# Weights enter the conversion at 0.8 chunks a slot, in place of 0.4, while the first eight heads run alone

## The chip, the cores and the metric

The kernel runs on one core of a Trainium2 chip. The metric is the device time of one execution in microseconds (us); lower is better. Times are given as the median of several runs.

## What is computed

Causal attention with a gate of cumulative sums for 4 batches of 8 heads (576 positions, head dimension 64), then two dense two-layer blocks on the 2304 resulting tokens (512 to 2048 to 512 each). All matrices arrive as 64-bit or 32-bit floats, and the result is asked for in near-float32 accuracy.

```python
scores = scale * q @ k.T + minimum(-(cum[:, None] - cum[None, :]), 0)   # causal
x = softmax(scores) @ v                          # 4 x 8 heads -> 2304 x 512
h = x @ w1_in;  x = (h * clip(h + 3, 0, 6) / 6) @ w1_out
h = x @ w2_in;  y = (h * sigmoid(h)) @ w2_out
```

## The kernel before

**Heads.** Attention is cut into 64 parts, called heads here: the first 256 rows ("A") or the rest ("B") of one head of one batch. The first 22 are handled "whole" (L484, L503, L516, L546, L610, L617, L628): scores on PE (tiles ps0, ps1), mask and row minimum on DVE into pb0 and pb1 (L503), exponential on ACT (L516), transposes on PE (pt, L546), a copy on ACT (th), the product with the values on PE (po, L610), normalizing on DVE (L617), and for each pair of heads a transpose back (px, L628) and a copy to xA on DVE (L107). The inputs of the first 14 heads lie in SBUF places that weights take over later (`spare`).

**Steps.** The first dense block runs in steps. Step i (counted from 0) makes one 128-wide slice of h for 256 tokens in `first` (12 matmuls, L239 to L241, into ph, of which there is one buffer), gates it in `gate_high` and `gate_low` (ACT L251, DVE L252, a copy to gh at L107, DVE L259), and adds its share to the sums in `second` (12 matmuls, L278 to L280). The L252 of a step is called its gate here: it is the last reader of ph, so the next step's `first` can't begin before it. Gate 1 is that of step 0. The first 16 steps use heads 0 to 7.

**Weights.** Each weight matrix comes as 16 chunks of 512 KB (128 x 512 numbers of 64 bits), 32 for the first block, in the order i0, o0, i1, o1, and so on. A chunk passes the `Feed`: load by DMA (L132), two ACT instructions (`fields`, L144 and L145), three on DVE (`join`, L153, L157, L160), a rounding copy on ACT (`high`, L105) and a subtraction on DVE (`low`, L171). Step i needs i chunk number i in `first` and o chunk number i one step later in `second`. After the L171 of its chunk a weight is ready. One `tick` moves each chunk in the feed one stage further and loads one more.

**Order of the work.** The program is written as a plan of slots. Slots 0 to 8 hold heads only (eight heads, and a ninth slot that finishes them); from slot 9 on a slot holds a step, and nearly always a head. In each slot `rate` chunks enter the feed: `feed_at` gathers the fraction over the four places of a slot where `ticks` stands, and its whole part is ticked. Three ticks are made before slot 0. A scheduler then sets the order of each engine's instructions with its own idea of their costs, so the program's order only leads it: steps and heads of different slots are interleaved. Each engine runs its own instructions strictly in the order it was given.

```python
for i in range(4):
    feed_at += rate / 4
    tk[i] = int(feed_at)
    feed_at -= tk[i]
slot(cur, p1, p2, nx, loads, has_step, tk)
```

Of the kernel before, what the change touches and what calls it, by code (L numbers as in the profile page):

```python
# [27 lines left out]
def kernel(  # L28
# [17 lines left out]
    B, H, D, S = qT.shape  # L46
# [281 lines left out]
    def split_rows():  # L328

        def row(tag, name):  # L330
            return wpool.tile([BH, S], F32R, tag=tag, name=name)

        f = NF - 1
        hi, lo = row(f"i{f}", "cumh"), row(f"o{f}", "cuml")
        one, neg = row(f"i{NF // 2 - 2}", "one"), row(f"o{NF // 2 - 2}", "neg")
        nc.gpsimd.memset(f32(one), 1.0)
        nc.gpsimd.memset(f32(neg), -1.0)
        nc.scalar.copy(hi, crow)
        nc.vector.tensor_tensor(out=lo, in0=crow, in1=f32(hi), op=ALU.subtract)
        for r, t in enumerate((one, one, hi, lo, neg, neg)):  # L340
            nc.sync.dma_start(f32(rows_d[:, r, :]), f32(t))
# [294 lines left out]
    def split1(blk):  # L636

        n = sizes[blk][1]
        b, a, _ = blocks[blk][0]
        xhs, xls = [], []  # L640
        for c in range(NDC):
            xh = xpool.tile([P, n], F32R, tag=f"xh{c}", name=f"xh{blk}_{c}")
            xl = xpool.tile([P, n], F32R, tag=f"xl{c}", name=f"xl{blk}_{c}")
            srcs = [((xB if a else xA)[b, c], slice(0, T1))]
            if n > T1:
                srcs += [(xZ[c], slice(T1, n))]
            for src, o in srcs:
                nc.scalar.copy(xh[:, o], src)
                nc.vector.tensor_tensor(
                    out=xl[:, o], in0=src, in1=f32(xh[:, o]), op=ALU.subtract  # L650
                )
            xhs.append(xh)
            xls.append(xl)
        xsplit[blk] = [(xhs, xls)]
# [39 lines left out]
    def slot(cur, p1, p2, nx, loads, mm, tk=(0, 0, 0, 0)):  # L694

        nonlocal step
        ng = len(p1.groups) if p1 else 0
        npc = len(cur.pieces) if cur else 0

        def scores(i):  # L700
            if i < npc:
                cur.score(i)
                cur.soft(i)

        def exps(i):
            if i < npc:
                cur.expo(i)

        def transposed(i):
            if i < ng:  # L710
                p1.trans(i)
                p1.trans_low(i)

        scores(0)
        scores(1)
        exps(0)
        if p2:
            p2.av_sum()
        ticks(tk[0])
        if mm:  # L720
            first(step, 0)
        if p1:
            p1.v_high()
        exps(1)
        scores(2)
        if nx:
            nx.qk_high()
        transposed(0)
        if p1:
            p1.v_low()  # L730
        exps(2)
        if cur:
            cur.load_v()
        if nx and npc <= 3:
            nx.qk_low()
        ticks(tk[1])
        if mm:
            first(step, 1)
            gate_high(step)
        scores(3)  # L740
        if nx and npc > 3:
            nx.qk_low()
        exps(3)
        for hd in loads:
            hd.load()
        transposed(1)
        if cur:
            cur.norm()
        ticks(tk[2])
        if mm:  # L750
            second(step - 1, 0)
        transposed(2)
        if mm:
            gate_low(step)
        transposed(3)
        ticks(tk[3])
        if nx:
            nx.places()
        for hd in loads:
            hd.load_cum()  # L760
        if mm:
            second(step - 1, 1)
        if p1:
            p1.av()
        if mm:
            step += 1

    def at(i):
        return heads[i] if 0 <= i < len(heads) else None
# [13 lines left out]
    nslot = 0  # L783
    for has_head, has_step in plan:
        cur = at(k) if has_head else None
        nx = at(k + 1) if has_head else None
        loads = []
        while has_head and loaded < len(heads) and loaded <= k + (
            2
        ):  # L790
            loads.append(heads[loaded])
            loaded += 1
        k += has_head and cur is not None
        tk = [0, 0, 0, 0]
        if not feed.done():
            rate = ((0.4,)*9+(2,))[min(nslot, len(((0.4,)*9+(2,))) - 1)]
            for i in range(4):
                feed_at += rate / 4
                tk[i] = int(feed_at)
                feed_at -= tk[i]  # L800
        slot(cur, p1, p2, nx, loads, has_step, tk)
        if nslot == 2:
            split_rows()
        p1, p2 = cur, p1
        nslot += 1
        if nslot == H + 1:
            p2.av_sum()
            p2 = None
            split1(0)
            turns["s"] = turns["s"][:1]  # L810
        if has_step and step in first_step[1:NB1]:
            blk = first_step.index(step)
            assert k - (cur is not None) >= (blk + 1) * H
            if p2:
                p2.av_sum()
                p2 = None
            if blk == NB1 - 1:
                cx.close()
                xpool = c0.enter_context(
                    tc.tile_pool(name="xlast", bufs=1, side="right", reuse_waits="tile")  # L820
                )
            split1(blk)
            if blk == NB1 - 1:
                break
# [335 lines left out]
```

## Time and profile before

| | us |
|---|---|
| median of 3 runs (lowest, highest) | 1031.37 (1030.43, 1031.85) |
| profiled execution, its time | 1032.36 |
| profiled execution, its span (first to last instruction) | 1030.6 |
| PE busy in the span | 993.1 (96%) |
| weight loads of PE (PEld) | 921.9 (89%) |
| DVE busy | 720.5 (70%) |
| ACT busy | 523.4 (51%) |
| POOL busy | 204.8 (20%) |

The shares are means over stages that differ. In the first 150 us heads, weights and steps run side by side; after that PE has hardly a gap up to 600 us. All times in the trace count from the first instruction. A matmul's end is modelled, so the distance from one start to the next tells how fast PE really goes; on DVE, too, the next instruction often starts before the last one's end, and the distance of starts is the cost of one more instruction.

### The profile page before, as it was taken

How to read it: one execution, taken by the hardware profiler on the slowest of the kernel's cores; microseconds unless marked ns; L12 is line 12 of the kernel's file. 1: busy time of each engine (PE TensorE's matmuls, PEld its weight loads, DVE VectorE, ACT ScalarE, POOL GpSimd, SP SyncE). 2: the span in 40 equal slices, each digit the busy share in tenths (PEclk: the TensorE clock that was granted, in tenths of full speed). 3: DMA queues.
4: the chain of work that ended last, by engine and by line, in shares of the span. 5: the costliest groups of instructions: out<-in, count | busy, mean ns of one | idle time of the engine just before them, and what ended most of it. 6: DMA issues, size and time to landing. Idle time of an engine off the chain costs nothing.

```text
span 1030.6 us, 18218 instructions
## 1 busy us (share of the span) xinstructions
PE 993.1 (96%) x6322; PEld 921.9 (89%) x6322; DVE 720.5 (70%) x1794; ACT 523.4 (51%) x1138; POOL 204.8 (20%) x378
## 2 busy tenths in 40 slices
PE   4988999999999999999999999999999999999996
PEld 3878899999999999999998887789988899889895
DVE  6699986888788878888728896977574334743342
ACT  5697744555456666656516563755353223432232
POOL 5000033443245444444401231000000000000000
PEclk9999999999999999999999999999999999999999
DMA  4793131222222322321114956343354332442412
GB/s 151 210 339 122 48 93 43 57 75 59 87 61 63 88 68 62 88 73 56 52 41 143 375 218 225 121 174 132 126 188 165 127 143 81 175 154 81 143 72 61
DMA packets 51907, 124.78 MB, mean 121 GB/s; under 512 B 9972, under 2 KB 31464, under 8 KB 48488
## 3 DMA queue, kind: packets, MB, share of 16 engines
q1 hardware_dynamic: 51816, 123.63, 36.0%
q8 instruction: 50, 0.82, 0.3%
q14 instruction: 41, 0.34, 0.1%
HBM read 98.96 MB, written 24.63 MB: 120 GB/s over the span
## 4 chain that ended last, share of the span: by engine, by line
PE 85%; DVE 7%; DMA 3%; ACT 1%; POOL 1%; issue 1%; SPq 1%; DVEq 0%; POOLq 0%; ACTq 0%
PE ph L239 6%; PE ph L240 6%; PE a L981 6%; PE ph L241 6%; PE a L982 6%; PE a L983 6%; PE acc L279 6%; PE acc L280 6%; PE acc L278 6%; PE h L965 5%; PE h L967 5%; PE h L966 5%; PE poB L595 4%; PE pt0B L546 1%; DMA out_dram<-o 1%; PE pt1B L546 1%
## 5 line engine op out<-in xcount | busy, mean ns | idle before, releaser
L239 PE MATMUL ph<-xh,wi 128*128 128x256 f32 (+1 forms) x512 | 155.4, 304 | 6.0 <-DVE g L252 5.9
L279 PE MATMUL acc<-gl,wo 128*128 128x256 f32 (+1 forms) x512 | 153.5, 301 | 0.4 <-DVE gl L259 0.2
L240 PE MATMUL ph<-xl,wi 128*128 128x256 f32 (+1 forms) x512 | 153.1, 299 | 0.0
L241 PE MATMUL ph<-xh,wi 128*128 128x256 f32 (+1 forms) x512 | 152.9, 299 | 0.0
L280 PE MATMUL acc<-gh,wo 128*128 128x256 f32 (+1 forms) x512 | 151.2, 297 | 0.0
L278 PE MATMUL acc<-gh,wo 128*128 128x256 f32 (+1 forms) x512 | 146.0, 301 | 0.1
L1010 ACT ACTIVATE gh<-h 128x384 fp32r<-128x384 f32 x96 | 50.4, 525 | 177.7 <-DVE h L1018 177.5
L981 PE MATMUL a<-wo,gh 128*128 128x512 f32 x288 | 113.1, 393 | 2.4 <-ACT gh L1010 2.4
L982 PE MATMUL a<-wo,gh 128*128 128x512 f32 x288 | 113.1, 393 | 0.0
L239 PEld LDWEIGHTS ph<-xh,wi 128*128 128x128 f32 x512 | 98.3, 192 | 11.1 <-DVE g L252 6.6
L240 PEld LDWEIGHTS ph<-xl,wi 128*128 128x128 f32 x512 | 98.7, 193 | 2.9
L279 PEld LDWEIGHTS acc<-gl,wo 128*128 128x128 f32 x512 | 96.9, 189 | 4.8 <-DVE gl L259 1.4
L241 PEld LDWEIGHTS ph<-xh,wi 128*128 128x128 f32 x512 | 98.5, 192 | 2.8
L280 PEld LDWEIGHTS acc<-gh,wo 128*128 128x128 f32 x512 | 96.7, 189 | 3.7
L278 PEld LDWEIGHTS acc<-gh,wo 128*128 128x128 f32 x512 | 96.0, 189 | 4.3 <-DVE gh L107 0.4
L983 PE MATMUL a<-wo,gl 128*128 128x512 f32 x288 | 90.4, 395 | 0.0
L251 ACT ACTIVATE g<-ph,half 128x512 f32<-128x512 f32 (+1 forms) x80 | 51.3, 643 | 63.7 <-PE ph L241 63.1
L1012 DVE TENSOR_TENSOR gl<-h,gh 128x384 fp32r<-128x384 f32 x96 | 53.5, 557 | 40.7 <-ACT h L1011 38.7
L252 DVE SCALAR_TENSOR_TENSOR g<-g,ph 128x512 f32<-128x512 f32 (+1 forms) x80 | 50.5, 633 | 40.1 <-ACT g L251 39.9
L1018 DVE TENSOR_TENSOR h<-h,u 128x384 f32<-128x384 f32 x72 | 40.1, 557 | 53.1 <-PE h L967 52.7
L99 POOL TENSOR_SCALAR gh<-g 128x512 fp32r<-128x512 f32 x64 | 50.8, 794 | 126.0 <-DVE g L252 112.7
L965 PE MATMUL h<-x0t,w 128*128 128x384 f32 x192 | 65.6, 342 | 0.7 <-DVE u L1018 0.7
(224 smaller groups left out, 2563.3 us busy)
## 6 DMA issues: line engine op xcount, KB each, us to landing
w<-w_d SPq DMA_DIRECT2D x18, 1792.0 KB
w_d<-w SPq DMA_DIRECT2D x8, 1792.0 KB
k2B<-in_kT_dram SPq DMA_DIRECT2D x64, 144.0 KB
rawi<-in_w1i_dram SPq DMA_DIRECT2D x16, 512.0 KB
rawo<-in_w1o_dram SPq DMA_DIRECT2D x16, 512.0 KB
rawi<-in_w2i_dram SPq DMA_DIRECT2D x16, 512.0 KB
rawo<-in_w2o_dram SPq DMA_DIRECT2D x16, 512.0 KB
q2B<-in_qT_dram SPq DMA_DIRECT2D x64, 80.0 KB
```

Of the source, the lines that this page charges most:

```text
L239: nc.tensor.matmul(o, wih[:, cs], xh[c], start=c == 0, stop=False)
L240: nc.tensor.matmul(o, wih[:, cs], xl[c], start=False, stop=False)
L241: nc.tensor.matmul(o, wil[:, cs], xh[c], start=False, stop=c == NDC - 1)
L278: nc.tensor.matmul(a, woh[:, cs], gh[:, jj, :], start=b0, stop=False)
L279: nc.tensor.matmul(a, woh[:, cs], gl[:, jj, :], start=False, stop=False)
L280: nc.tensor.matmul(a, wol[:, cs], gh[:, jj, :], start=False, stop=b1)
L965: nc.tensor.matmul(ps, w[:, 0, cs], xh[:, c, :], start=c == 0, stop=False)
L966: nc.tensor.matmul(ps, w[:, 0, cs], xl[:, c, :], start=False, stop=False)
L981: nc.tensor.matmul(accs[t], gh[:, k, cs], woh, start=b0, stop=False)
L982: nc.tensor.matmul(accs[t], gh[:, k, cs], wol, start=False, stop=False)
L983: nc.tensor.matmul(accs[t], gl[:, k, cs], woh, start=False, stop=b1)
L1012: nc.vector.tensor_tensor(out=gl[:, i, o], in0=g, in1=f32(gh[:, i, o]), op=ALU.subtract)
```

## The change

```diff
         if not feed.done():
-            rate = ((0.4,)*9+(2,))[min(nslot, len(((0.4,)*9+(2,))) - 1)]
+            rate = 0.8 if nslot <= H else 2
             for i in range(4):
```

H is 8, so slots 0 to 8 are meant in both versions, and from slot 9 on the rate is 2 in both. In nine slots 0.4 gives 3.6, that is 3 ticks; 0.8 gives 7.2, that is 7. By slot 9 the feed has made 10 ticks in place of 6, and every chunk from the fourth on stands earlier in the program. No instruction is added or taken away; the scheduler's order changes on all engines up to about the 1500th of 6100 PE instructions and is the same behind that.

**DVE around gate 1.** Names carry the chunk or head before the tile's number. Before:

```order
L153 SCALAR_TENSOR_TENSOR rawi_5_688<-rawi_5_688 128x512
L171 TENSOR_TENSOR wi_4_811<-magi_4_726,wi_4_811 128x512
L157 TENSOR_SCALAR magi_5_813<-magi_5_813 128x512
L160 ISA mago_4_768<-rawo_4_640,mago_4_768 128x1024
L252 SCALAR_TENSOR_TENSOR g_542<-g_542,ph_522 128x256
L503 ISA pb0A_5_830,mxA_5_829<-ps0A_5_845,cmask 128x128
```

And with the change:

```order
L160 ISA mago_6_826<-rawo_6_693,mago_6_826 128x1024
L171 TENSOR_TENSOR wi_6_862<-magi_6_777,wi_6_862 128x512
L153 SCALAR_TENSOR_TENSOR rawo_7_784<-rawo_7_784 128x512
L503 ISA pb0A_5_874,mxA_5_873<-ps0A_5_889,cmask 128x128
L503 ISA mxA_5_873 128x1
L252 SCALAR_TENSOR_TENSOR g_586<-g_586,ph_555 128x256
```

The gate comes after the same 13 heads, but after the 13th L171 (i6) in place of the 9th (i4). Counted over all DVE instructions ahead of gate 1, the change has 5 more L153, 3 L157, 4 L160, 4 L171 and one 128-wide L503.

**DVE around gates 11 and 12, where the conversion ends.** Before, ahead of gate 12 (step 11):

```order
L160 ISA magi_14_1603<-rawi_14_1492,magi_14_1603 128x1024
L171 TENSOR_TENSOR wo_13_1632<-mago_13_1562,wo_13_1632 128x512
L617 TENSOR_TENSOR xtA_2_1481<-poA_3_1543,sums_96 128x2x64
L252 SCALAR_TENSOR_TENSOR g_1513<-g_1513,ph_1494 128x256
L430 TENSOR_TENSOR qsA_6_1718<-q2A_6_1593,qsA_6_1718 64x256
```

With the change, around gate 11 (step 10):

```order
L160 ISA mago_15_1612<-rawo_15_1508,mago_15_1612 128x1024
L523 TENSOR_SCALAR sums_92<-sums_92 128x2
L259 TENSOR_TENSOR gl_1298<-g_1296,gh_1297 128x256
L617 TENSOR_TENSOR xtA_2_1525<-poA_3_1583,sums_96 128x2x64
L252 SCALAR_TENSOR_TENSOR g_1385<-g_1385,ph_1352 128x256
L524 RECIPROCAL sums_92<-sums_92 128x2
L171 TENSOR_TENSOR wo_15_1678<-mago_15_1612,wo_15_1678 128x512
```

The same head work (xtA_2, from head 3 of the third batch) stands one gate earlier, and the last chunk, o15, is done right behind gate 11, where before only 25 of the 32 chunks are done by gate 11. Between gates 1 and 11 the change has on DVE 3 more 256-wide and 2 more 128-wide L503, 3 L523, 4 L524, 2 L617, 2 copies to xA, 2 casts to qs and 4 subtractions at L430 and L431, and of the conversion 5 fewer L153, and 1 L157, 1 L160 and 3 L171 more.

**SP, the loads of heads 3 and 4.** inA is the place of a head's inputs. Before:

```order
L399 DMA inA_2_157<-orow 1x16x16
L389 DMA inA_3_184<-in_qT_dram 64x256
...
L399 DMA inA_3_184<-orow 1x16x16
L389 DMA inA_4_217<-in_qT_dram 64x256
...
L132 DMA rawo_1_228<-in_w1o_dram 128x1024
L398 DMA inA_4_217<-cum_d 1x256
```

With the change (a line of dots stands for the head's other loads, here as above):

```order
L399 DMA inA_2_157<-orow 1x16x16
L132 DMA rawo_1_180<-in_w1o_dram 128x1024
L389 DMA inA_3_189<-in_qT_dram 64x256
...
L399 DMA inA_3_189<-orow 1x16x16
L132 DMA rawi_2_228<-in_w1i_dram 128x1024
L389 DMA inA_4_230<-in_qT_dram 64x256
...
L398 DMA inA_4_230<-cum_d 1x256
```

One chunk's load now stands ahead of head 3's loads, and two stand ahead of head 4's first.

## Rows read from the trace of the kernel before

**Rows 1.** Windows by stage: us of each engine busy (instructions), granted clock, DMA share, GB/s.

```profile
20.00:45.00 25.00, 23.95 (x96) 20.89 (x95) 15.18 (x62) 14.89 (x43) 0.00 (x0) 1.00 0.59 176
45.00:58.20 13.20, 12.34 (x48) 10.79 (x47) 13.04 (x41) 12.71 (x33) 0.00 (x0) 1.00 0.99 321
58.20:114.40 56.20, 50.01 (x349) 46.60 (x350) 56.20 (x162) 46.40 (x106) 4.35 (x14) 0.94 0.53 181
114.40:121.60 7.20, 6.30 (x55) 6.05 (x54) 7.18 (x26) 6.07 (x18) 0.87 (x1) 1.00 0.23 63
121.60:145.30 23.70, 22.23 (x183) 21.26 (x181) 21.95 (x71) 14.16 (x35) 4.94 (x8) 1.00 0.24 65
145.30:250.00 104.70, 104.70 (x870) 103.94 (x871) 80.83 (x236) 53.63 (x134) 45.03 (x79) 1.00 0.23 63
```

**Rows 2.** Timeline of PE: start, duration, instruction; neighbours at 60 and at 66 us.

```profile
60.12 0.41 PE L239 MATMUL ph<-xh,wi 128*128 128x256 f32 x1
60.34 0.41 PE L240 MATMUL ph<-xl,wi 128*128 128x256 f32 x1
...
66.04 0.28 PE L239 MATMUL ph<-xh,wi 128*128 128x256 f32 x1
66.16 0.28 PE L240 MATMUL ph<-xl,wi 128*128 128x256 f32 x1
```

**Rows 3.** Timeline of DVE around gate 1; the L252 is gate 1.

```profile
56.66 0.69 DVE L171 TENSOR_TENSOR wi<-magi,wi 128x512 fp32r<-128x512 f32 x1
57.27 0.43 DVE L157 TENSOR_SCALAR magi<-magi 128x512 int32<-128x512 int32 x1
57.60 0.69 DVE L160 CUSTOM_DVE_ANT_0 mago<-rawo,mago 128x1024 uint16<-128x1024 uint16 x1
58.20 0.42 DVE L252 SCALAR_TENSOR_TENSOR g<-g,ph 128x256 f32<-128x256 f32 x1
58.53 0.29 DVE L503 CUSTOM_DVE_ANT_0 pb0A<-ps0A,cmask 128x128 f32<-128x128 f32 x1
...
58.74 0.70 DVE L153 SCALAR_TENSOR_TENSOR rawo<-rawo 128x512 int32<-128x512 int32 x1
59.34 0.17 DVE L523 TENSOR_SCALAR sums<-sums 128x2 f32<-128x2 f32 x1
59.41 0.43 DVE L503 CUSTOM_DVE_ANT_0 pb1A<-ps1A,cmask 128x256 f32<-128x256 f32 x1
59.76 0.09 DVE L503 DVE_READ_ACCUMULATOR2_ANT mxA<- 128x1 f32 x1
```

**Rows 4.** Timeline of DVE: gate 11.

```profile
114.41 0.45 DVE L252 SCALAR_TENSOR_TENSOR g<-g,ph 128x256 f32<-128x256 f32 x1
```

**Rows 5.** Groups of ACT, 20 to 58.2 us: count, busy us, mean ns, idle before.

```profile
L144 ACT ACTIVATE rawo<-rawo 128x512 int32<-128x512 uint32 x5 | 3.4, 677 | 1.1 <-DMA rawo<-in_w1o_dram 1.1
```

**Rows 6.** Timeline of SP: the load of a weight chunk.

```profile
17.96 0.43 SPq L132 DMA_DIRECT2D rawo<-in_w1o_dram  x1
```

**Rows 7.** Waits of PE, whole span, for a gate: total us, times, longest.

```profile
PE ph L239 <- DVE g L252: 5.9, 7, 1.8
```

**Rows 8.** Timeline of PE: first matmuls of steps 11 and 17.

```profile
115.83 0.37 PE L239 MATMUL ph<-xh,wi 128*128 128x256 f32 x1
...
145.30 0.36 PE L239 MATMUL ph<-xh,wi 128*128 128x256 f32 x1 [0.27 <-DVE g L252]
```

**Rows 9.** Waits of PE, 114 to 150 us, columns as in rows 7.

```profile
PE pxA L628 <- DVE xtA L617: 0.9, 1, 0.9
PE ph L239 <- DVE g L252: 0.8, 2, 0.5
PE ps0A L492 <- DVE qsA L430: 0.4, 1, 0.4
PE acc L279 <- DVE gl L259: 0.2, 1, 0.2
```

**Rows 10.** Windows of 2 us, columns as in rows 1.

```profile
72.00:74.00 2.00, 2.00 (x12) 2.00 (x10) 2.00 (x6) 1.29 (x3) 0.00 (x0) 0.50 0.90 323
90.00:92.00 2.00, 2.00 (x12) 1.97 (x11) 2.00 (x8) 0.90 (x3) 0.00 (x0) 0.61 0.41 166
```

## The prediction, made before the changed kernel ran

> **What bounds the kernel now.** I read the windows by stage first [rows 1]. The reader is to see three regimes. From 20 to 45 us PE is busy 23.95 of 25.00 us and DVE only 15.18: the heads run alone and PE sets the pace. From 45 to 114 us DVE is full (13.04 of 13.20, then 56.20 of 56.20): the conversion of the weights, the heads and the steps meet there. From 145 us PE has no gap in 104.70 us. So whatever this change gives or takes must show before 145 us, and from there PE carries it to the end unchanged.
>
> PE's own pace in the first regime has to be read from the distance of starts [rows 2]. The column of the granted clock says 1.00 there, but at 60 us two 128x256 matmuls start 0.22 us apart, and at 66 us 0.12 us. The heads thus run at the lower of the two clock levels, 1.2 GHz, which is why a stage with so little in it fills PE.
>
> Then come the steps' gates. Gate 1 stands at 58.20 [rows 3], gate 11 at 114.41 [rows 4]. Ten gates take 56.2 us on a DVE without a gap.
>
> **What the change moves.** It does what it says: 13 chunks are converted ahead of gate 1 in the new order, 9 in the old. The cost of each instruction on DVE is the distance to the next start [rows 3]: L171 0.61, L157 0.33, L160 0.60, L153 0.60, the L503 of 128 columns 0.21 and of 256 columns 0.35, L523 0.07, L252 0.33.
>
> *Ahead of gate 1.* 5 x 0.60 + 3 x 0.33 + 4 x 0.60 + 4 x 0.61 + 0.21 = 9.0 us more on DVE. Between 20 and 58.2 us DVE was busy 15.18 + 13.04 = 28.22 of 38.20 us [rows 1], so 9.98 us lie idle, and with the change 37.2 of 38.2 are taken. ACT was busy 14.89 + 12.71 = 27.60; it gets about 12 more instructions of the conversion (three stages of four chunks), at most 0.68 each [rows 5], so at most 35.8. PE was busy 36.29. The idle time of DVE is therefore the cover for the moved work, and it just suffices, with three engines at 94 to 97%.
>
> Let d be the delay of gate 1. At the least DVE is the bound with no gap at all, and gate 1 comes 1.0 us earlier (d = -1.0). At the most nothing is hidden and d = 9.0. My value is near the low end, for the nearest row to a stage with full DVE is 45 to 58.2 us, and there PE still was busy 12.34 of 13.20, so it lost 6.5% against 4.2% between 20 and 45. That much over 25 us is 0.6 us. To this come two loads of weights that now stand ahead of the loads of heads 3 and 4 on SP, 0.43 us each [rows 6], 0.9 us, hidden only if those loads landed early; and 0.5 us, half of what DVE has left, for ACT's fuller queue. Sum: d = 2.0.
>
> *From gate 1 to gate 11.* DVE is full in both versions. By the counts of the two orders the change has there 3 x 0.35 + 2 x 0.21 + 3 x 0.07 + 4 x 0.07 + 2 x 0.21 for heads (L617 priced like the narrow L503) and 8 x 0.33 for copies, casts and subtractions (priced like L252), together 5.0, and for the conversion -5 x 0.60 + 0.33 + 0.60 + 3 x 0.61 = -0.2. So 4.8 us more: three more heads are fitted in, and the conversion stays as dense as it was, only further ahead. Gate 11 falls at 58.2 + d + 56.2 + 4.8 = 119.2 + d. **The steps come later in the middle, not earlier**: where `first` waited before, it was for the gate on DVE, 7 times [rows 7], and for no weight.
>
> *From gate 11 on* the conversion is over, where before seven more chunks were still to finish (4 L157, 5 L160, 7 L171, 8.6 us). Here DVE's cover is gone and PE sets the pace alone. Before, step 11 began at 115.83 and step 17 at 145.30 [rows 8], 29.5 us for 207 matmuls of the PE order, of which 2.3 us were waits, all for DVE [rows 9]. Without those it is 27.2 us, 0.131 a matmul. The change has 211 matmuls between the same two places: 27.6 us, from 119.6 + d (0.4 for the gate itself) to 147.2 + d. But at its step 17 it has done 28 matmuls more, those of one B head, 3.7 us at that pace, so it compares with 149.0 before. The balance is 1.8 us gained, less d.
>
> *After that* the order evens out and PE is full in both; I count nothing. The sum with d = 2.0: +0.2 us on the profiled execution's own 1032.36 (its span 1030.6 and 1.8 around it). The median of the runs lies 1.0 lower, at 1031.37, and gives 1031.6.
>
> One rule speaks against the change. What the rows show: after PE had stood waiting for gates, the granted clock fell to 0.50 and 0.61 in two places [rows 10], down to the 1.2 GHz level; there the 12 matmuls of a `first` cost 12 x (0.22 - 0.12) = 1.2 us more [rows 2], hidden so far because DVE was the bound. The Trainium skill, "TensorE: Matmul & The Clock Gate", section "What's actually happening", says that the throttled state is the default and that activity releases it. By that rule a PE that waits 4.8 us longer for its gates would fall back once more, and if that lasted past gate 11 the sum would be 1032.8 in place of 1031.6. The trace agrees that the clock falls after waits, but both its places lie well before gate 11, so my sum leaves it out.
>
> **The rivals.**
> 1. *The early heads jam* (slower). DVE, ACT and PE at 94 to 97% each, in fixed orders that the scheduler made with other costs, wait for each other: a chunk's L153 that stands ahead of a head's L503 holds up the head, and PE with it. Price: d itself, all of which stays, less 1.8. It decides from d = 3.9 (2.1 us slower, 0.2%); d = 5 gives 1034.6, d = 7 1036.6, d = 9 1038.6. For it: PE is cold and has no spare in 20 to 58 us. Against it: DVE's work is spread in pieces of 0.6 us, and scores run two heads ahead of the transposes.
> 2. *The cover holds fully* (faster). d = -1.0, a DVE without a gap from 20 us on: 1.8 + 1.0 = 2.8 us gained, 1028.6. For it: 45 to 58.2 us shows DVE at 99%. Against it: there PE had a lead, and it must feed DVE every head.
> 3. *The DVE time is worth its full price* (much faster). 8.6 us of conversion leave the stretch in which DVE is full, and the end moves by as much: 1022.8. Against it: PE has only 2.3 us of waits after gate 11 to give up [rows 9], and the order spends the room between the gates on heads.
>
> **How the numbers follow.** A measurement of this kernel tells about 0.2%, 2.1 us, from no change. My forecast, no change that can be measured, holds for d from -0.3 to 3.9: 0.46. Rival 1 beyond 3.9: 0.36, of which 0.04 for d somewhat below 3.9 with a fallen clock past gate 11. Rival 2: 0.15; rival 3: 0.03. The range runs from rival 2's 1028.6 to d = 7, 1036.6; outside are rival 3 and the last part of rival 1.
>
> **What would show it.** Gate 1 at about 60.2 us (58.2 and 62.1 bound the forecast); DVE busy over 90% between 20 and 58 us; gate 11 near 121 us, later than before; the last L171 near 122 us; no wait of PE for DVE between gate 11 and step 17, and step 17 near 149 us. I am wrong if gate 1 stands beyond 63 us, if PE waits after gate 11 for something that DVE had hidden (a load of a B head, POOL), or if gate 11 comes before 114 us.

## The result and the profile after

The change makes the kernel slower: 1036.36 us, median of eight runs (1035.71 to 1042.82), against 1031.26 us for the kernel before (eight runs, 1029.88 to 1032.59). The ratio is 1.0058, with a 95% interval of 1.0048 to 1.0068. The forecast was 1031.6 us; the measured time lies at the upper end of the range.

The profile that came with this result is of the slowest of the eight executions (1042.82 us). The rows below therefore come from a second profile of the same kernel, of an execution of 1036.94 us; its runs are the experiment e_again.

| us | before | after |
|---|---|---|
| profiled execution | 1032.36 | 1036.94 |
| its span | 1030.6 | 1035.2 |
| PE busy | 993.1 | 993.3 |
| DVE busy | 720.5 | 720.8 |
| ACT busy | 523.4 | 522.5 |

All engines do the same work in 4.6 us more. The windows by stage show where; each stage is cut at the places that were used before, gate 1 at 61.1, gate 11 at 125.2, the start of step 17 at 155.2 (columns as in rows 1).

```profile
20.00:45.00 25.00, 22.48 (x90) 19.80 (x88) 20.52 (x74) 18.72 (x54) 0.00 (x0) 1.00 0.69 202
45.00:61.10 16.10, 14.60 (x57) 12.69 (x57) 15.56 (x47) 15.77 (x38) 0.00 (x0) 1.00 0.99 315
61.10:125.20 64.10, 55.75 (x375) 52.20 (x376) 61.93 (x190) 49.22 (x118) 5.45 (x17) 0.89 0.42 140
125.20:155.20 30.00, 28.27 (x235) 27.61 (x234) 25.24 (x79) 15.68 (x42) 9.37 (x17) 1.00 0.23 65
155.20:250.00 94.80, 94.80 (x793) 94.17 (x792) 65.85 (x191) 44.96 (x110) 35.34 (x63) 1.00 0.19 55
```

Against [rows 1] the stretch from gate 1 to gate 11 has grown from 56.2 to 64.1 us. VectorE, full before (56.20 of 56.20, 162 instructions), now makes 190 instructions there in 61.93 us, and stands idle for 2.2. The granted clock of the stretch is 0.89 in place of 0.94. From 155 us on PE is full, as before.

The waits of PE in that stretch have changed their kind. This is the view of waits from 61.1 to 125.2 us:

```profile
PE acc L279 <- DVE gl L259: 2.8, 4, 1.5
PE acc L278 <- DVE gh L107: 2.2, 2, 2.0
PE poA L610 <- ACT th0A L105: 1.5, 3, 0.9
PE ps1A L484 <- DVE mxA L503: 1.0, 1, 1.0
```

Before, PE waited in `first` for the last step's gate [rows 7]. Now it waits in `second` for gh and gl of the gate, and in the heads. Three of these four waits end with an instruction of DVE, whose queue now holds more. Before, the stretch from 58.2 to 114.4 us has

```profile
PE ph L239 <- DVE g L252: 5.1, 5, 1.8
```

and 0.8 us behind one copy on ACT, 5.9 us in all; the four lines of the changed kernel add up to 7.5. DVE itself, without a wait before, now waits, most of it here (view of DVE's waits, 61.1 to 125.2 us):

```profile
DVE sums L523 <- ACT pb1A L516: 1.1, 2, 0.7
```

The places that the prediction named, first in the timeline of DVE (gate 1, the last L171 of the first block, gate 11), then in that of PE (a wait behind gate 11, and the first matmul of step 17):

```profile
61.14 0.42 DVE L252 SCALAR_TENSOR_TENSOR g<-g,ph 128x256 f32<-128x256 f32 x1
...
120.17 0.67 DVE L171 TENSOR_TENSOR wo<-mago,wo 128x512 fp32r<-128x512 f32 x1
...
125.23 0.42 DVE L252 SCALAR_TENSOR_TENSOR g<-g,ph 128x256 f32<-128x256 f32 x1 [0.45 <-ACT g L251]
```

```profile
149.05 0.36 PE L239 MATMUL ph<-xh,wi 128*128 128x256 f32 x1 [1.73 <-DVE g L252]
...
155.25 0.28 PE L239 MATMUL ph<-xh,wi 128*128 128x256 f32 x1
```

The last gate of all (L252 has 80) stands at 627.2 us before and at 633.5 after, so 6.3 us are lost by then. Behind it the kernel before takes 403.4 us and the changed one 401.7: 1.7 us come back in the second block. Some 1.4 of them are the clock's: in the kernel before it fell there (0.83 granted from 645 to 655 us), in the changed kernel it did not (1.00 from 651.3 to 661.3), and the same matmuls, from the first L981 to the L965 behind the L983, take 4.74 us (646.51 to 651.25) before and 3.33 (652.20 to 655.53) after.

### The profile page after: what moved, and what is told of

Same layout as the page of the kernel before. It is cut to its first block, busy times and chain, and to the rows that moved or that the text cites. A ratio compares the mean times of both kernels' runs of the same rounds, so it can differ in the third digit from the quotient of the medians.

```text
span 1041.0 us, 18218 instructions
## 1 busy us (share of the span) xinstructions
PE 991.0 (95%) x6322; PEld 919.7 (88%) x6322; DVE 721.4 (69%) x1794; ACT 521.9 (50%) x1138; POOL 199.6 (19%) x378
## 4 chain that ended last, share of the span: by engine, by line
PE 83%; DMA 8%; DVE 4%; SPq 2%; ACT 1%; POOL 1%; issue 1%; DVEq 0%; ACTq 0%; POOLq 0%
PE ph L239 6%; PE ph L240 6%; PE ph L241 6%; PE acc L279 6%; PE acc L280 6%; PE acc L278 6%; PE a L981 6%; PE a L982 6%; PE a L983 6%; PE h L965 5%; PE h L966 5%; PE h L967 5%; PE poB L595 4%; DMA rawo<-in_w1o_dram 3%; DMA rawi<-in_w1i_dram 2%; PE pt0B L546 1%
## 5 line engine op out<-in xcount | busy, mean ns | idle before, releaser
L981 PE MATMUL a<-wo,gh 128*128 128x512 f32 x288 | 113.1, 393 | 1.7 <-ACT gh L1010 1.7
L983 PE MATMUL a<-wo,gl 128*128 128x512 f32 x288 | 89.9, 393 | 0.5 <-DVE gl L1012 0.5
L252 DVE SCALAR_TENSOR_TENSOR g<-g,ph 128x512 f32<-128x512 f32 (+1 forms) x80 | 50.3, 630 | 45.9 <-ACT g L251 45.4
L99 POOL TENSOR_SCALAR gh<-g 128x512 fp32r<-128x512 f32 x64 | 46.9, 733 | 135.7 <-DVE g L252 124.3
L965 PE MATMUL h<-x0t,w 128*128 128x384 f32 x192 | 65.2, 340 | 0.7 <-DVE u L1018 0.7
```

What stands on the lines that cost most here:

```text
L965: nc.tensor.matmul(ps, w[:, 0, cs], xh[:, c, :], start=c == 0, stop=False)
L981: nc.tensor.matmul(accs[t], gh[:, k, cs], woh, start=b0, stop=False)
L983: nc.tensor.matmul(accs[t], gl[:, k, cs], woh, start=False, stop=b1)
```

## The experiments

In each diff the line with the minus is the changed kernel's, or the one before's where that is said. A table behind the last one has every run.

### The same kernel again

No edit.

> The changed kernel once more, for a second profile: the first profiled execution (1042.8 us, granted clock 0.975) lies 6 us above the kernel's other executions, so it may show more than the change. Theory of the jam (DVE, ACT and PE hold each other up while the first heads run): 1036 us, gate 1 at 62 to 65 us (58.2 before), granted clock near 0.99. Theory of the clock (the loss is PE at its lower level): gate 1 may differ between executions, and the time goes with the granted clock: 1042 at 0.975, 1036 only where it is 0.99.

1036.70 us, ratio 1.0055 [1.0036, 1.0074]. The loss repeats; its profile is the one above. The time does not go with the mean clock of an execution: the fastest of the four, 1034.13 us, shows 0.979, the slowest, 1040.02 us, 0.992.

### Other placements of the ticks: e_late, e_early, e_mid

```diff
-            rate = 0.8 if nslot <= H else 2
+            rate = ((0,)*3 + (1.2,)*6 + (2,))[min(nslot, 9)]    # e_late
+            rate = ((0.8,)*4 + (0,)*5 + (2,))[min(nslot, 9)]    # e_early
+            rate = ((0.6,)*9 + (2,))[min(nslot, 9)]             # e_mid
```

> Rate 0 in slots 0 to 2, 1.2 in slots 3 to 8: 7 ticks before slot 9 as in the change, but no chunk's load ahead of the inputs of heads 3 and 4. 12 chunks are converted ahead of gate 1 in the order (13 in the change, 9 before). Theory of the loads (PE waits for inputs behind weights on SP, 3 us of it in the changed kernel's trace): 1031 to 1033 us. Theory of the jam: as the change, 1035 to 1038 us, since as many chunks must go between the first heads.

> Rate 0.8 in slots 0 to 3, 0 in slots 4 to 8: 3 ticks before slot 9 as in the kernel before, but chunks o1 and i2 loaded ahead of the inputs of heads 3 and 4 as in the change. 6 chunks ahead of gate 1 (which the order also puts two heads earlier). Theory of the loads: 1034 to 1036 us. Theory of the jam: 1029 to 1032 us, as before or better.

> Rate 0.6 in slots 0 to 8: 5 ticks before slot 9. Theory of the jam: half of the change's loss, 1033 to 1034 us. Theory of the loads (only o1 ahead of head 4's inputs): 1031 to 1033 us. If the scheduler's order, not the rate, makes the time, no line: anything from 1028 to 1037 us.

Measured: e_late 1035.27 us (1.0036 [1.0023, 1.0048]), e_early 1037.37 (1.0054 [1.0037, 1.0072]), e_mid 1035.79 (1.0036 [1.0023, 1.0050]). My first two theories fell here. The jam gave e_late its time (1035 to 1038 had been expected), but e_mid lies above what it gave and e_early far above. e_late puts no load of a chunk ahead of heads 3 and 4, and its PE is busy 7.41 us up to 20 us and 23.42 from 20 to 45, as before (7.47, 23.95); still it loses 4.5 us (with 3.5 us in two waits of PE for inputs of heads at 46 and 51 us, which the other placements do not show at that size). e_early has three ticks in these slots, as the kernel before, only earlier, and loses as much as the change with its seven; one of its eight executions, though, took 1030.55 us, the other seven 1036.54 to 1038.91. So neither the loads on SP nor the number of chunks ahead of gate 1 carries the loss.

### The rates next to 0.4: e_r35, e_r45

```diff
-            rate = 0.8 if nslot <= H else 2
+            rate = ((0.35,)*9 + (2,))[min(nslot, 9)]    # e_r35
+            rate = ((0.45,)*9 + (2,))[min(nslot, 9)]    # e_r45
```

> The kernel before with 0.35 in place of 0.4 in slots 0 to 8: three ticks there as at 0.4, a few places later each, and again 9 chunks and 13 heads ahead of gate 1. Theory of the amount (what counts is how many chunks are ahead of gate 1): same as before, 1030 to 1032 us. Theory of the order (the order that 0.4 happens to give leaves PE little to wait for, and any other placement of the ticks loses 4 to 6 us whatever its amount): 1034 to 1037 us.

> The kernel before with 0.45 in place of 0.4 in slots 0 to 8: four ticks in place of three, 10 chunks and 13 heads ahead of gate 1 (before 9 and 13, with 0.8 13 and 13). Theory of the amount: a quarter of the change's loss at the most, 1031 to 1033 us. Theory of the order: 1034 to 1037 us.

Measured: 1032.78 us (1.0019 [1.0010, 1.0028]) and 1032.46 us (1.0015 [1.0005, 1.0024]). Neither theory gets this fully: the amount explains 0.45 and just misses 0.35, and a redrawn order costs 1.5 us here, not 4 to 6. A change of 1 to 2 us can thus come from the scheduler's order alone; the 5 us of 0.8 are more than that.

### VectorE relieved: e_p8, e_p4

```diff
-        copy("v" if blk == 0 else "p", gh, g)
+        copy("p", gh, g)
```

e_p8 is this edit on the changed kernel (0.8), e_p4 the same on the kernel before (0.4).

> The changed kernel (0.8), with the 16 copies of g to gh in steps 0 to 15 on POOL in place of DVE; POOL is idle up to 60 us and busy under 2 us of each 20 up to 120. Theory of the full VectorE (between gates 1 and 12 DVE is the bound, and PE's 2.9 us of lost work from 60 to 120 us come from it): 16 x 0.33 = 5.3 us less on DVE give those 2.9 us back, 1032 to 1034 us. Theory of the order: the loss is in waits between engines and in PE's order, DVE's share does not matter, 1035 to 1038 us, a slower POOL copy ahead of second included.

> The kernel before (0.4), with the 16 copies of g to gh in steps 0 to 15 on POOL in place of DVE. Theory of the full VectorE: before's 2.8 us of PE idle from 60 to 100 us... 5.3 us less on DVE, 1027 to 1030 us. Theory of the order: DVE's relief is worth nothing by itself and the order is redrawn again, 1031 to 1036 us.

Measured: 1029.99 us (0.9988 [0.9979, 0.9996]) and 1030.14 us (0.9993 [0.9985, 1.0002]). The whole loss of 0.8 is gone, and more than the 2.9 us that I had expected at most; at 0.4 the same relief is worth about 1 us, not clear of noise and just short of the 1027 to 1030 that had been expected. Rate 0.8 and rate 0.4 are then equal. The windows of e_p8 and e_p4 from their gate 1 to their gate 11, one kernel each:

```profile
62.60:119.80 57.20, 50.45 (x375) 47.83 (x375) 56.67 (x165) 47.00 (x112) 9.97 (x25) 0.97 0.45 156
```

```profile
58.20:115.50 57.30, 49.50 (x366) 45.64 (x366) 57.00 (x159) 48.25 (x110) 15.23 (x25) 1.00 0.52 180
```

In e_p8 PE does the same 375 matmuls between the two gates as in the changed kernel, in 57.2 us in place of 64.1. Gate 1 itself is no earlier (62.6), so what happens ahead of gate 1 is not what costs the 5 us. (POOL is not idle up to 60 us, as the expectation has it: it is busy for 13.22 us of the first 20 in the changed kernel.)

### The dose the other way, another relief, another placement: e_d4, e_l8, e_pmid, e_h8

e_d4 is the kernel before with the copy made twice on DVE:

```diff
-        copy("v" if blk == 0 else "p", gh, g)
+        copy("v" if blk == 0 else "p", gh, g); blk == 0 and copy("v", gh, g)
```

> The kernel before (0.4), in which DVE makes the copy of g to gh twice in steps 0 to 15: 16 x 0.33 = 5.3 us more on DVE, some 10 of the 16 between gates 1 and 11. Theory of the full VectorE: there DVE has no gap and PE little to spare, so about 3 to 5 us are lost, 1034 to 1037 us. Theory of the order: the dose on DVE does not count by itself, a redrawn order costs what 0.35 and 0.45 cost, 1032 to 1033 us.

e_l8 is the changed kernel with the subtraction of `gate_low` on POOL:

```diff
-        nc.vector.tensor_tensor(out=gl, in0=g, in1=f32(gh), op=ALU.subtract)
+        (nc.gpsimd if flat[i][1] == 0 else nc.vector).tensor_tensor(out=gl, in0=g, in1=f32(gh), op=ALU.subtract)
```

> The changed kernel (0.8) with the subtraction of gate_low, L259, on POOL in steps 0 to 15 in place of the copy of gh: as many us off DVE as with the copy on POOL (1030.0), in another place of the chain and in another order. Theory of the full VectorE: 1029 to 1032 us. Theory of the order (the copy on POOL met a lucky order): 1034 to 1037 us.

e_pmid joins the edit of e_mid to that of e_p8; e_h8 puts only the copies of steps 0 to 7 on POOL, at 0.8:

```diff
-        copy("v" if blk == 0 else "p", gh, g)
+        copy("v" if 8 <= i < 16 else "p", gh, g)
```

> 0.6 in slots 0 to 8 (1035.8 us by itself), with the copies of gh of steps 0 to 15 on POOL. Theory of the full VectorE: with DVE relieved the placement of the ticks no longer counts, 1029 to 1032 us. Theory of the order: 1034 to 1037 us, as without POOL.

> The changed kernel (0.8), with the copies of gh on POOL in steps 0 to 7 alone and on DVE in steps 8 to 15; DVE's order is that of the run with all 16 on POOL up to gate 11. Theory of the full VectorE: the relief counts between gates 1 and 11, where 8 of 10 copies are taken off DVE, and most of the 6.4 us come back, 1030 to 1032.5 us. Theory that the relief counts later or in all 16 alike: half comes back, 1033 to 1034 us. Theory of the order: 1034 to 1037 us.

Measured: e_d4 1036.86 us (1.0053 [1.0041, 1.0065]), e_l8 1031.51 (1.0007 [0.9996, 1.0018]), e_pmid 1034.16 (1.0019 [1.0002, 1.0035]), e_h8 1029.88 (0.9984 [0.9976, 0.9993]). Three of the four came out as the theory of the full VectorE had it, e_h8 a little better. Put 5.3 us on DVE and the kernel before loses as much as by the change; take them off in another way and the change loses next to nothing; take off only those of the first eight steps and everything comes back. The stretch between gates 1 and 11 of e_d4, and then of e_h8:

```profile
58.60:119.30 60.70, 53.15 (x362) 49.25 (x362) 60.70 (x185) 49.73 (x117) 4.62 (x15) 0.92 0.48 172
```

```profile
61.70:118.20 56.50, 49.99 (x374) 46.47 (x375) 56.44 (x169) 46.91 (x111) 8.59 (x23) 1.00 0.45 156
```

Both times DVE is full to the last tenth, and its work is the length of the stretch. e_h8 against the changed kernel: 374 matmuls for 375, 169 DVE instructions for 190. Eight of these 21 are the copies. The rest is conversion and head work that now stands behind gate 11, for in this order the gates stand further ahead: the groups of DVE in the stretch have 9 of the wide L503 and 17 of L171 here, 10 and 19 there. So the relief acts twice, and the runs do not part the two. POOL's side of it in e_h8, from 58 to 120 us (columns as in rows 5):

```profile
L99 POOL TENSOR_SCALAR gh<-g 128x256 fp32r<-128x256 f32 x8 | 4.3, 532 | 70.5 <-DVE g L252 68.0 <-PE pt0A L546 2.4
```

Eight copies of 0.53 us on an engine that, with them, is busy for 8.59 us of the 56.50.

e_pmid missed: 1034.2, not 1029 to 1032. There the order begins the steps earlier (gate 1 at 50.4 us, with 10 heads and 7 chunks ahead of it, 13 and 13 in the changed kernel), and PE's longest waits between 50 and 113 us are for inputs of heads and for weights, which the relief of DVE did not remove:

```profile
PE ps0A L484 <- DMA k2A<-in_kT_dram: 2.0, 2, 1.8
...
PE ph L239 <- ACT wi L105: 1.3, 1, 1.3
```

One of its nine executions took 1026.49 us, the shortest of all that were measured, the other eight 1033.13 to 1035.71.

### The clock, the heads, a fourth placement: e_f8, e_s8, e_plate

e_f8 fills PE's waits with spare matmuls:

```diff
-            phs[i] = pool.tile([P, len(fs), n], F32, tag="ph", name=f"ph{i}")
+            phs[i] = pool.tile([P, 2 if blk == 0 else len(fs), n], F32, tag="ph", name=f"ph{i}")
...
-        ph = phs.pop(i)
+        two = phs.pop(i); ph = two[:, : len(fs), :]; [nc.tensor.matmul(two[:, 1, :], W['i', m, fs[0]][0][:, 0:P], xsplit[blk][0][0][c], start=True, stop=True) for c in range(4 if blk == 0 and i <= 10 else 0)]
```

> The changed kernel (0.8) with four spare 128x256 matmuls on PE in each of steps 0 to 10, behind the step's first, into a half of ph's bank that nothing reads; the output is unchanged. 44 matmuls, 44 x 0.12 = 5.3 us at the higher clock. Theory of the clock (the loss is the time at the lower clock level between 66 and 125 us that PE's waits for DVE bring about; before 7 us of it, with 0.8 14 us, without it in the runs at 1030 and below): PE's waits are filled, the windows from 60 to 140 us show 1.00, and 3 to 6 us come back against at most 2 us that the spare matmuls cost where PE did not wait, 1032 to 1035 us. Theory of the full VectorE alone (DVE's time between the gates is lost whatever the clock): nothing comes back, and the spare matmuls cost up to 3 us, 1036 to 1039 us.

1038.94 us (1.0080 [1.0067, 1.0093]). The windows of 20 us from 60 to 140:

```profile
60.00:80.00 20.00, 17.14 (x111) 16.13 (x109) 20.00 (x51) 17.16 (x38) 1.39 (x4) 1.00 0.84 308
80.00:100.00 20.00, 14.72 (x97) 13.65 (x95) 16.43 (x48) 12.54 (x31) 1.12 (x4) 0.83 0.37 120
100.00:120.00 20.00, 19.16 (x158) 18.40 (x157) 20.00 (x65) 15.48 (x40) 2.96 (x7) 1.00 0.16 45
120.00:140.00 20.00, 20.00 (x171) 19.77 (x171) 15.48 (x59) 8.97 (x28) 2.66 (x6) 1.00 0.28 78
```

A mean granted clock of 0.83 over 20 us is 2 x 0.17 x 20 = 6.8 us at 1.2 GHz; the changed kernel shows 0.83, 0.91, 1.00 and 0.91 in these four windows, 14 us. So half of the time at the lower level was gone, and the kernel was 2.2 us slower for it, not 3 to 6 us faster. The clock alone is not the loss. The test is not a clean one, since it did not hold the clock up throughout and adds work to PE, 5.3 us by the expectation's own count.

e_s8 sets heads back in the plan:

```diff
-    plan = [(True, False)] * (H + 1) + [(i in [0,1,2,3,4,5,6,7,8,9,10,12,14,*range(16,58)], True) for i in range(72)]
+    plan = [(True, False)] * (H + 1) + [(i in [0,2,4,6,7,8,9,10,11,12,13,14,15,*range(16,58)], True) for i in range(72)]
```

> The changed kernel (0.8) with the heads set further back in the plan: the slots with steps 1, 3 and 5 have no head, those of steps 11, 13 and 15 have one; by gate 11 VectorE's order holds 21 heads in place of 23, and 31 chunks in place of 32. Theory of the full VectorE: two heads and a chunk fewer, some 5 us of DVE, between gates 1 and 11, gate 11 at 118 to 121 us in place of 125, and most of the loss comes back, 1030 to 1033 us. Rival (the heads only change places with other work of PE and DVE): 1035 to 1038 us.

1034.83 us (1.0039 [1.0025, 1.0052]; runs from 1032.27 to 1037.31): between the two. In the profiled execution, the fastest of them, the stretch took 58.1 us, gate 11 stood at 120.5, as expected, and the time was 1032.27. Over all runs only 1.9 us came back, and this one stays unclear.

e_plate joins the edit of e_late to that of e_p8.

> No tick in slots 0 to 2 and 1.2 a slot in slots 3 to 8 (1035.3 us by itself), with the copies of gh of steps 0 to 15 on POOL. Theory of the full VectorE: 1029 to 1032 us, as at 0.8 and 0.4. If 0.6 with POOL (1034.2) is the rule and 0.8 with POOL (1030.0) a lucky order: 1033 to 1036 us.

1030.66 us (0.9996 [0.9987, 1.0005]). With e_p8, e_p4 and this one, three placements out of four give 1030 to 1031 us once DVE is relieved, and 0.8 with POOL was no lucky order.

### Which of the sixteen steps: e_g8, e_h4

```diff
-        copy("v" if blk == 0 else "p", gh, g)
+        copy("v" if i < 8 else "p", gh, g)
```

> The other half: the changed kernel (0.8) with the copies of gh on DVE in steps 0 to 7 and on POOL in steps 8 to 15. DVE's order up to gate 8 is that of the changed kernel. Theory of the full VectorE between gates 1 and 11: of the ten copies there only two are taken off DVE (0.7 us), so 0.5 to 1.5 us come back, 1034.5 to 1036.5 us. Theory that the relief counts in all 16 steps alike, or that any change to the copies meets a luckier order: 1030 to 1033.5 us.

1038.32 us (1.0078 [1.0061, 1.0095]). The other half of the same relief brings nothing: the time lies above both ranges, where 0.5 to 1.5 us had been expected back. The stretch shortened to 60.7 us, gate 11 at 123.0, but behind it PE then waited for a gate on DVE, here in the view of waits from 123 to 153.4 us:

```profile
PE ph L239 <- DVE g L252: 3.2, 2, 2.9
```

So it is the first eight steps that count, and a shorter stretch is no gain where a wait behind it takes it back.

e_h4 is the edit of e_h8 on the kernel before.

> The kernel before (0.4) with the copies of gh on POOL in steps 0 to 7 alone. Theory of the full VectorE: with DVE relieved between gates 1 and 9 the rate counts for nothing, as with all 16 (1030.1 at 0.4, 1030.0 at 0.8, and 1029.9 at 0.8 with steps 0 to 7): 1029 to 1031 us. Rival (0.8 with the relief is really faster than 0.4 with it, since its conversion is over earlier): 1030.5 to 1032 us here.

1032.02 us (1.0012 [1.0003, 1.0021]), 2 us above e_h8 and at the end of the rival's range; my own theory missed. With all sixteen copies on POOL the two rates were equal (1030.14 and 1029.99 us), so it is open whether this is a gain of the early conversion. It is about as large as the differences that 0.35 and 0.45 showed between orders, and the relief was not quite the same: a copy on POOL took 1016 ns on the mean here, 532 in e_h8.

### All runs

The stretch is that from the profile's gate 1 to its gate 11, with DVE's busy time and PE's matmuls in it; the profiled execution is not always the median one.

| run | what | median us | ratio | profiled us | stretch us | DVE busy | matmuls |
|---|---|---|---|---|---|---|---|
| before | 0.4 | 1031.3 | 1 | 1032.4 | 56.2 | 56.2 | 349 |
| after | 0.8, first profile | 1036.4 | 1.0058 | 1042.8 | 70.3 | 62.7 | 386 |
| e_again | 0.8, second profile | 1036.7 | 1.0055 | 1036.9 | 64.1 | 61.9 | 375 |
| e_late | 0, then 1.2 | 1035.3 | 1.0036 | 1035.2 | 62.3 | 59.4 | 369 |
| e_early | 0.8, then 0 | 1037.4 | 1.0054 | 1037.6 | 64.9 | 63.9 | 378 |
| e_mid | 0.6 | 1035.8 | 1.0036 | 1036.1 | 62.9 | 62.6 | 389 |
| e_r35 | 0.35 | 1032.8 | 1.0019 | 1033.8 | 56.7 | 56.6 | 365 |
| e_r45 | 0.45 | 1032.5 | 1.0015 | 1032.5 | 56.8 | 56.7 | 367 |
| e_p8 | 0.8, gh on POOL | 1030.0 | 0.9988 | 1031.5 | 57.2 | 56.7 | 375 |
| e_p4 | 0.4, gh on POOL | 1030.1 | 0.9993 | 1030.9 | 57.3 | 57.0 | 366 |
| e_d4 | 0.4, gh twice on DVE | 1036.9 | 1.0053 | 1036.3 | 60.7 | 60.7 | 362 |
| e_l8 | 0.8, gl on POOL | 1031.5 | 1.0007 | 1033.9 | 59.6 | 57.3 | 375 |
| e_pmid | 0.6, gh on POOL | 1034.2 | 1.0019 | 1035.7 | 62.3 | 60.0 | 375 |
| e_h8 | 0.8, gh on POOL in steps 0 to 7 | 1029.9 | 0.9984 | 1030.4 | 56.5 | 56.4 | 374 |
| e_f8 | 0.8, 44 spare matmuls | 1038.9 | 1.0080 | 1038.5 | 64.1 | 59.6 | 407 |
| e_s8 | 0.8, heads set back | 1034.8 | 1.0039 | 1032.3 | 58.1 | 56.6 | 365 |
| e_plate | 0, then 1.2, gh on POOL | 1030.7 | 0.9996 | 1032.4 | 57.6 | 56.6 | 376 |
| e_g8 | 0.8, gh on POOL in steps 8 to 15 | 1038.3 | 1.0078 | 1038.2 | 60.7 | 60.3 | 377 |
| e_h4 | 0.4, gh on POOL in steps 0 to 7 | 1032.0 | 1.0012 | 1032.0 | 57.3 | 57.0 | 353 |

Read by its own profiled time, every execution with a stretch under 59 us ends below 1034 us, and every one with more than 60 above 1035. For e_early, e_mid and e_pmid the length is not like for like: their gate 1 stands at 53.7, 50.6 and 50.4 us, so the stretch holds other work, and gate 11 of e_mid and e_pmid (113.5 and 112.7) comes before that of the kernel before. What costs these two their time is not shown.

## Why the prediction was wrong

The forecast gave a value for each piece of the way; against the second profile of the changed kernel they stand as follows.

| step of the sum | forecast | measured |
|---|---|---|
| d, delay of gate 1 | 2.0 (bounds -1.0 and 9.0) | 61.14 - 58.20 = 2.9 |
| gate 1 to gate 11 | 56.2 + 4.8 = 61.0 | 64.1 |
| gate 11 to step 17 | 28.0, no wait of PE for DVE | 30.0, one wait of 1.7 |
| balance behind step 17 | +0.2 | 633.5 - 627.2 = +6.3 |
| after that | 0 | -1.7 |
| span | +0.2 | 1035.2 - 1030.6 = +4.6 |

**Gate 1 was right.** The cover of 9.98 us of idle DVE held: nine us of conversion more cost 2.9 us, within the bounds and below the 3.9 from which rival 1 was to decide. In it is one wait of 1.98 us of PE, at 18.63 us, for inputs whose loads now stand behind weights; the forecast had 0.9 for that. e_h8 has the same wait (1.90 us) and ends at 1029.9. From 20 us to gate 1 DVE was 88% busy (20.52 + 15.56 of 41.10 us), not over 90. So the early heads did not jam, in the rival's sense, and e_p8, e_h8 and e_plate, with gate 1 as late as 61.5 to 62.6 us, end at 1030 to 1031. What the change does ahead of gate 1 is worth little at the end. That the measured time still lies inside the range is luck: its upper end was drawn for d = 7, for a loss ahead of gate 1, and the loss came behind it.

**Gate 1 to gate 11 is the step that failed.** Its mechanism was right: DVE is full there, and the extra heads in its queue make the ten gates longer. The size was not: 64.1 in place of 61.0. Of the 3.1 us that were missing, 0.9 are DVE work (61.93 busy against 61.0 counted) and 2.2 are idle time of DVE, which the forecast had at nothing. It took for granted that a queue that was full in the order before stays without a gap in another order; in the new one PE's `second` waits for gh and gl, and DVE in its turn for ACT (L523 1.1 us behind the exponentials, L171 0.2) and for PE (L617 0.3). e_d4 shows the price of DVE time there without any change of the feed: 10 copies more between the gates, and the head work that the longer gates let in, make the stretch 4.5 us longer and the kernel 5.6 us slower. e_h8 shows it from the other side: eight copies less, and the stretch with the same PE work is 56.5 us again.

**Behind gate 11 the forecast was too kind as well.** It let PE run alone, at 0.131 us a matmul and without a wait. There were 28.27 us busy of 30.00, and one wait of 1.73 us for a gate. The weight of the 28 matmuls that are already done at step 17, 3.7 us, was right: 155.25 less the 149.0 that it was to be compared with is 6.25, and 6.3 is what is missing at the last gate. The three errors, 0.9, 3.1 and 2.0, make up, to rounding, the 6.1 us between the forecast balance and the measured one.

**Why it does not come back.** The kernel before also has the same conversion to do, only later; but later is where DVE has room. From 114.4 to 145.3 us [rows 1] it did 29 us of DVE work beside a PE that was busy 28.5 of 30.9. The change does some 14 us of DVE work more before gate 11 (the prediction's 9.0 and 4.8), where PE depends on it, and leaves DVE with idle time behind gate 11, where PE is full and can't go faster: 25.24 of 30.00 us, then 65.85 of 94.80 (before 80.83 of 104.70). That was my argument against rival 3, and it held; I did not see that it speaks against the forecast too.

**The rule that was left out.** The rows show that the clock did fall further: 0.89 over 64.1 us is 14 us at 1.2 GHz between gates 1 and 11, against 0.94 over 56.2 us, 7 us. The Trainium skill, "TensorE: Matmul & The Clock Gate", section "What's actually happening", says that the throttled state is the default and that activity releases it. The trace agrees only in part: in the kernel before PE still ran at the lower level at 60 us [rows 2], although it had been busy for 36.29 of the 38.20 us ahead of gate 1 [rows 1]. Taking it in would have moved the forecast by 1.2 us to 1032.8, still 3.6 short. And e_f8, with half as much time at the lower level, was slower. Nor does the clock of the stretch put the runs in order: it is 0.97 in e_g8 (1038.2 us) and 0.95 in e_mid (1036.1), but 0.94 in e_plate and in the kernel before (1032.4 both). In e_h8 and e_p4, two of the three fastest, the clock shows 1.00 in all windows from 60 to 160 us, so there the short waits and the high clock go together; which part of the 5 us is the clock's is not settled, only that it does not explain them alone.

**What stays open.** Why 0.6 with the relief keeps 3 us of its loss, and why setting heads back gave so little in most runs. Why the relief of steps 0 to 7 brings nothing at 0.4, and why e_g8, with a stretch 3.4 us shorter, is no faster. How one execution each of e_early and e_pmid could be 6 and 7 us faster than the rest, in the same fixed order; neither was profiled. Orders with the same load differ by 1 to 2 us, and no run here resolves that.

**A version that beats both:** e_h8, the changed kernel with the copies of gh on POOL in steps 0 to 7, at 1029.88 us, 0.16% below the kernel before (0.07 to 0.24%). That the gain over the changed kernel comes from the relief of VectorE is shown; whether the faster feed has a part in the gain over the kernel before is not. e_p4, with all sixteen copies on POOL at the old rate, is within 0.3 us of e_h8, but the same eight copies at the old rate give 1032.02 us (e_h4).

## What to carry to other kernels

Where one engine is full in a stretch and another is full behind it, work moved ahead on the first is not free because it would have been done later anyway: it delays the second engine where that can't run ahead, and the idle time that it leaves later is of no use. Count what stands on the full engine between two fixed points of the chain, and expect that a new order may have gaps on top of it. And before shifting the work of a full engine in time, look for one with room: eight copies of 0.53 us on POOL gave back all that the faster feed had cost. At the old rate the same eight gave nothing, so the relief has to be tried in the order in which it is to be used.

## What the runs showed of the hardware

The same copy of 128x256 numbers on POOL took 542 ns on the mean in e_p8 and 935 ns in e_p4, from 58 to 120 us, with DVE full in both (56.67 of 57.20 us and 57.00 of 57.30 between the gates); the two groups, of e_p8 and then of e_p4:

```profile
L99 POOL TENSOR_SCALAR gh<-g 128x256 fp32r<-128x256 f32 x10 | 5.4, 542 | 73.9 <-DVE g L252 73.9
```

```profile
L99 POOL TENSOR_SCALAR gh<-g 128x256 fp32r<-128x256 f32 x11 | 10.3, 935 | 74.9 <-DVE g L252 70.7 <-DVE xtA L617 2.6 <-DVE sums L523 1.6
```

In e_h4, the other kernel at 0.4, it took 1016 ns, in e_h8 532. What stretches it was not tried. I had also not expected how far two executions of one program with one fixed order can part: the stretch took 64.1 us in one profile of the changed kernel and 70.3 in the other, with 61.9 and 62.7 us of DVE work in it, so most of the difference is idle time on DVE:

```profile
62.00:132.30 70.30, 55.94 (x386) 52.49 (x387) 62.67 (x190) 49.03 (x118) 5.43 (x16) 0.87 0.41 135
```

In the two profiles the column of the granted clock also differs ahead of gate 1: from 34 to 66 us it shows 0.50 in the first and 1.00 in the second, while PE goes at the same pace (six matmuls of L610 take 1.38 us in both, at 40.62 and at 40.20 us). So the column can miss the lower level there, as the prediction read from the distance of starts.

The eight runs of the changed kernel spread over 7.1 us, those of the kernel before over 2.7. Slow orders do not all spread so: the five runs of e_d4 lie within 1.5 us.
